# Pooled attention and two dense stages on one core: copy and load order on the DMA queue, GpSimd's split order, two tiles transposed in fp32

## The chip, the cores and the metric

The kernel runs as one program on one core of a Trainium2 chip. The metric is the device time of one execution in microseconds; the number to predict is the median of several executions of the changed kernel, and of the kernel before three executions are known.

## What is computed

The reference is a chain of three layers on float32 inputs. Only the first one is touched by the change.

```python
def _attn_ref(q, k, v):                       # q, k, v: (2, 8, 1152, 64)
    B, H, S, D = q.shape
    factor = 2
    scale = 1.0 / np.sqrt(D)
    q_pool = q.reshape(B, H, S // factor, factor, D).mean(axis=3)
    scores = scale * np.matmul(q_pool, k.transpose(0, 1, 3, 2))
    scores = scores - np.max(scores, axis=-1, keepdims=True)
    attn = np.exp(scores)
    attn = attn / (np.sum(attn, axis=-1, keepdims=True) + 1e-09)
    return np.matmul(attn, v).astype(np.float32)
...
    x = _moe_ref(x=x, **moe_kwargs)           # x*tanh(softplus(x)) between two matmuls, 512 -> 2048 -> 512
    return _moe2_ref(x=x, **moe2_kwargs)      # 8 experts 512 -> 1024 -> 512, mixed by 8 Sinkhorn rounds
```

## The kernel before

The 16 heads are taken as 8 **pairs** of heads (`NPAIR`). A pair has 2 x 576 pooled queries, that is 9 **tiles** of 128 queries (`QTL`), and one turn of the loop at L665 is one **step** `g`: pair `p = g // 9`, step `t = g % 9` of the pair. fp32 precision is kept by splitting an operand into a rounded fp32r part ("hi") and the rest ("lo"), and by multiplying both.

A step has this chain over the engines. TensorE (PE) computes the scores of tile `g` (L448); VectorE (DVE) copies them, negated, out of the only score buffer in PSUM into a buffer `e` (3 of them) and finds the row maximum on the way (L453); ScalarE (ACT) takes the exponential in place (`exps`, L463). `hand_over(g)` (L465) then copies `e`, 128x1152 fp32, by DMA into a buffer `er` of type fp32r (2 of them). Three steps later (`LAG`) `transposes` turns `er` on PE in nine 128x128 blocks (L510), ACT writes the hi part (`eth`, L513) and DVE the lo part (`etl`, L516). Two to four tiles make a group, whose product with V is run in portions of 9 matmuls a step (L531). In order of the program, step `g` holds: the scores of `g`, GpSimd's preparations (`prep`), the first item of `turn(p, t)`, the transposes of tile `g - 3`, `hand_over(g - 1)`, the portion of the product with V, the other items of `turn`, and `exps(g)`. At its end come `loads` (L704), one entry of `late` (L706), and the weight work that is due (`run_all`).

The next pair's operands are prepared beside this. `prep(p, t)` issues GpSimd's (POOL's) work by the table `PREP` (L587): `q0` to `q3` pool, scale and split the next pair's queries, `v..` and `k..` split V and K, head by head, hi (`..0`) and lo (`..1`). A finished split appends the load of the next raw tile to `loads`, since it frees the raw tile's only buffer: `q3` the load of the queries, a lo split that of K or V. `trans_q(p, u)` turns split queries on PE (L428), ACT copies them to `qT` (L430), and `swap` (L418) writes by two DMAs the copy of `qT` with its two halves of partitions exchanged; the middle tile has a buffer of its own, `qz`, which is swapped too. When a pair's output is complete, `late` gets `scale_x(p)`: five transposes of the reciprocal row sums, two multiplications on DVE (L554), and on POOL the split of the pair's output `xs` into `xh` and `xl` (L560, L561), four instructions.

All DMAs are issued by SyncE (SP), one after the other in the order of the program. An issue that has to wait for another engine holds all later issues.

Steps 0 to 2 (`g < LAG`) are written apart (L672 to L680): they have no transposes, and the copies of tiles 0 and 1 are handed over in steps 1 and 2. From step 73 on (`T0`) the second layer's matmuls (L219, L752) run interleaved with the rest of the attention; after it follow the experts (L1013, L1171).

Of the kernel before, what the change touches and what calls it, by code (L numbers as in the profile page):

```python
# [8 lines left out]
F32 = mybir.dt.float32  # L9
F32R = mybir.dt.float32r  # L10
# [13 lines left out]
def pool_attention_mish_sinkhorn_kernel(  # L24
# [261 lines left out]
    with ExitStack() as actx:  # L286
# [37 lines left out]
        def heads(p):  # L324
            b, hp = divmod(p, HPB)
            return b, hp, 2 * hp
# [91 lines left out]
        def swap(t):  # L418

            for a, b in ((0, D), (D, 0)):  # L420
                nc.sync.dma_start(out=t[a:a + D, :, 1, :].bitcast(F32), in_=t[b:b + D, :, 0, :].bitcast(F32))

        def trans_q(p, u):
            ps = ps_t.tile([P, 4, P], F32R, tag="t", name=f"psq{p}_{u}")
            t, _ = q_tile(p, 4 * u)
            n = min(4, QTL - 4 * u)
            for i in range(n):
                nc.tensor.transpose(  # L428
                    ps[:, i, :], qst[p][:, 4 * u + i, 0:2, :].rearrange("p a d -> p (a d)"), identr)
            nc.scalar.activation(t[:, :, 0, :], ps[:, 0:n].bitcast(F32), AF.Copy)  # L430
            swap(t)
            if 4 * u == MID:
                middle(p, ps, 1)
                swap(qz[p % 2])

        scS, eS, erS, rsS, rxS = {}, {}, {}, {}, {}

# [19 lines left out]
        def exps(g):  # L457
            p, t = divmod(g, QTL)
            sc, nm = scS.pop(g)
            e = eS[g] = sc.rearrange("p a b -> p (a b)")  # L460
            if t == 0:
                rsS[p] = tiny.tile([P, QTL], F32, tag="rs", name=f"rs{p}", bufs=2)
            nc.scalar.activation(e, e, AF.Exp, bias=nm, scale=-1.0, accum_out=rsS[p][:, t:t + 1])  # L463

        def hand_over(g):  # L465

            e = eS.pop(g)
            er = erS[g] = er_p.tile([P, S], F32R, tag="er", name=f"er{g}")
            nc.sync.dma_start(out=er.bitcast(F32), in_=e)
# [26 lines left out]
        def transposes(g):  # L496
            p, t = divmod(g, QTL)
            e = erS.pop(g)
            q0 = t * P
            parts = []  # L500
            for gi, (j, s0, n) in enumerate(GROUPS):
                a, b = max(q0, s0), min(q0 + P, s0 + n)
                if a < b:
                    parts.append((get_et(p, gi), a - q0, b - q0, a - s0))
            for c3 in range(3):
                pt = ps_t.tile([P, 4, P], F32R, tag="t", name=f"psT{g}_{c3}")
                ps = pt.bitcast(F32)
                for i in range(3):
                    c = 3 * c3 + i
                    nc.tensor.transpose(pt[:, i, :], e[:, c * P:(c + 1) * P], identr)  # L510
                cs = slice(3 * c3, 3 * c3 + 3)
                for (eh, el), a, b, o in parts:
                    nc.scalar.activation(eh[:, cs, o:o + b - a], ps[:, 0:3, a:b], AF.Copy)  # L513

                for (eh, el), a, b, o in reversed(parts):
                    nc.vector.tensor_tensor(  # L516
                        out=el[:, cs, o:o + b - a], in0=ps[:, 0:3, a:b],
                        in1=eh[:, cs, o:o + b - a].bitcast(F32), op=ALU.subtract)
            for gi, (j, s0, n) in enumerate(GROUPS):
                if q0 < s0 + n <= q0 + P:  # L520
                    queue_av(p, gi)

        def queue_av(p, gi):
            j, s0, n = GROUPS[gi]
            eh, el = et.pop((p, gi))
            box = {}

            def mm(c, which):
                if "ps" not in box:
                    box["ps"] = ps_a.tile([P, 512], F32, tag="av", name=f"psA{p}_{gi}")  # L530
                nc.tensor.matmul(  # L531
                    box["ps"][:, 0:n], lhsT=vst[p, j][:, c].rearrange("p a d -> p (a d)"),
                    rhs=(el, eh)[which][:, c, 0:n],
                    start=(c == 0 and which == 0), stop=(c == NK - 1 and which == 1))

            def evac():
                ps = box["ps"]
                b, hp, h0 = heads(p)
                t = o_p.tile([D, SQ - c0], F32, tag="t", name=f"avt{p}_{gi}")
                nc.scalar.activation(t[:, 0:n], ps[D:2 * D, 0:n], AF.Copy)  # L540
                s = s0 - j * (SQ - D)
                nc.vector.tensor_tensor(
                    out=xs[j * D:(j + 1) * D, s:s + n], in0=ps[0:D, 0:n], in1=t[:, 0:n], op=ALU.add)
                if gi == len(GROUPS) - 1:
                    late.append(lambda: scale_x(p))

            def scale_x(p):
                for i0, n in ((0, 4), (4, 1)):
                    ps = ps_t.tile([P, n, P], F32, tag="t", name=f"psr{p}_{i0}", padded_shape=[P, 4, P])
                    rx = rxS[i0]  # L550
                    for i in range(n):
                        nc.tensor.transpose(ps[:, i, :], rx[:, i].rearrange("p a d -> p (a d)"), ident)
                    x = xs[:, i0 * P:(i0 + n) * P]
                    nc.vector.tensor_tensor(out=x, in0=ps.rearrange("p a b -> p (a b)"), in1=x, op=ALU.mult)  # L554
                b, hp, h0 = heads(p)
                sl = slice(b * SQ, (b + 1) * SQ)
                for j in range(2):
                    r = slice(j * D, (j + 1) * D)
                    x = xs[r, j * D:j * D + SQ]
                    split_hi(nc.gpsimd, xh[r, hp, sl], x)  # L560
                    split_lo(nc.gpsimd, xl[r, hp, sl], x, xh[r, hp, sl])  # L561

            for c in range(NK):
                for w in range(2):
                    av_todo.append(lambda c=c, w=w: mm(c, w))
            av_todo[-1] = lambda: (mm(NK - 1, 1), evac())
# [13 lines left out]
        for m in range(1, 2 * NG1 - 1):  # L580
# [4 lines left out]


        PREP = {  # L587
            "q0": 1, "q1": 2, "q2": 3, "q3": 5, "v00": 1, "v01": 2, "v10": 4, "v11": 7,
            "k00": 3, "k01": 4, "k10": 6, "k11": 8,
        }  # L590
        PREP0 = {"k00": 3, "k01": 3, "q0": 4, "q1": 4, "q2": 5, "q3": 5, "v10": 5, "v11": 7, "k10": 7, "k11": 8}
        TURN = {"k0": (5, 6, 7), "k1": (2, 3, 3), "k10": (0, 0, 2), "q0": (2, 2, 3), "q": (6, 1, 2)}
# [72 lines left out]
        for g in range(T0 + EARLY):  # L665
            p, t = divmod(g, QTL)
            if g == 1:
                bctx.close()
                ps_t = pool("ps_t", 4, space=PSUM)
                ps_a = pool("ps_a", 1, space=PSUM)  # L670
            pre = turn(p, t) if g < NQ else []
            if g < LAG:  # L672
                exps(g)
                for f in pre:
                    f()
                if g:
                    hand_over(g - 1)
                if g + 1 < LAG:
                    split_kv(0, 0, "v", nc.gpsimd, g)
                    scores(g + 2, ps_s)  # L680
            else:
                if LAG < g < NQ:
                    scores(g)
                if p and g < NQ:
                    prep(p, t)
                if g < T0:
                    run(g, "dve")
                if p and t == 1:
                    row_sums(p - 1)
                if pre:  # L690
                    pre.pop(0)()
                ready = len(av_todo)
                if g < NQ + LAG:
                    transposes(g - LAG)
                if g <= NQ:
                    hand_over(g - 1)
                if not p:
                    prep(p, t)
                run_av(min(ready, 9 if g < NQ else 18))
                for f in pre:  # L700
                    f()
                if g < NQ:
                    exps(g)
            while loads:  # L704
                loads.pop(0)()
            if late:  # L706
                late.pop(0)()
            if g < T0:
                run_all(g)
            if g == QTL:  # L710
                load_gate()
            if g == NQ - 1:
                sctx.close()
                ps_o = ctx.enter_context(tc.tile_pool(name="ps_o", bufs=3, space=PSUM, side="right"))
                wpools["d0"] = ctx.enter_context(tc.tile_pool(name="wd0", bufs=1, side="right"))
                mctx = ExitStack()
                wpools["d1"] = mctx.enter_context(tc.tile_pool(name="wd1", bufs=1, side="right"))
                wpools["t"] = mctx.enter_context(tc.tile_pool(name="wt2", bufs=3, side="right"))
            if g >= T0:
                mish_step(g - T0)  # L720
        run_av(len(av_todo))
        for f in late:
            f()


    wpools[1] = mctx.enter_context(tc.tile_pool(name="wb", bufs=1, side="right"))
# [540 lines left out]
```

## Time and profile before

| | us |
|---|---|
| median of 3 executions (1259.51 to 1262.87) | 1260.65 |
| the profiled execution, its own time | 1258.57 |
| its span, first to last instruction | 1256.8 |

The span is cut into windows below; the attention fills about its first 300 us, and PE is busy through nearly all of what follows. In the profile a wait is the idle time of an engine just before an instruction, put down to the engine and line that came last. [...]

### The profile page before, as it was taken

How to read it: one execution, taken by the hardware profiler on the slowest of the kernel's cores; microseconds unless marked ns; L12 is line 12 of the kernel's file. 1: busy time of each engine (PE TensorE's matmuls, PEld its weight loads, DVE VectorE, ACT ScalarE, POOL GpSimd, SP SyncE). 2: the span in 40 equal slices, each digit the busy share in tenths (PEclk: the TensorE clock that was granted, in tenths of full speed). 3: DMA queues.
4: the chain of work that ended last, by engine and by line, in shares of the span. 5: the costliest groups of instructions: out<-in, count | busy, mean ns of one | idle time of the engine just before them, and what ended most of it. 6: DMA issues, size and time to landing. Idle time of an engine off the chain costs nothing.

```text
span 1256.8 us, 19465 instructions
## 1 busy us (share of the span) xinstructions
PE 1217.6 (97%) x6872; PEld 1125.8 (90%) x6872; DVE 858.3 (68%) x1596; ACT 600.3 (48%) x1372; POOL 634.4 (50%) x737
## 2 busy tenths in 40 slices
PE   7988888999999999999999999999999999999998
PEld 7988888999999999988899999888888999998887
DVE  5877778887544433578876766866876667866865
ACT  6877778786755443352333333333233333333331
POOL 5445566433443433355865555555556654555552
PEclk9999999999999999999999999999999999999999
DMA  5876676653322211001111111011111111110112
GB/s 195 260 231 209 217 245 213 236 198 140 117 84 85 84 60 34 18 9 51 43 51 52 51 51 51 23 46 42 51 52 42 51 51 51 51 44 28 40 50 76
DMA packets 66417, 115.64 MB, mean 92 GB/s; under 512 B 6928, under 2 KB 39440, under 8 KB 66320
## 3 DMA queue, kind: packets, MB, share of 16 engines
q1 hardware_dynamic: 66320, 114.40, 28.5%
q8 instruction: 55, 0.90, 0.3%
q14 instruction: 42, 0.34, 0.1%
HBM read 64.50 MB, written 2.36 MB: 53 GB/s over the span
## 4 chain that ended last, share of the span: by engine, by line
PE 86%; DVE 4%; DMA 3%; POOL 3%; ACT 2%; issue 1%; SPq 0%; DVEq 0%; POOLq 0%; ACTq 0%
PE po L1171 29%; PE c L1013 25%; PE ph L219 10%; PE po L752 8%; PE psA L531 4%; PE psS L448 4%; DMA er<-e 3%; PE psT L510 2%; DVE e L453 2%; POOL xl L81 1%; DVE etl L516 1%; POOL qst L81 1%; POOL xh L78 1%; ACT eth L513 1%; ACT e L463 1%
## 5 line engine op out<-in xcount | busy, mean ns | idle before, releaser
L81 POOL TENSOR_TENSOR wslotsl<-s,wslotsh 128x256 fp32r<-128x256 f32 x180 | 132.9, 747 | 237.6 <-ACT wslotsh L74 237.6
L1179 DVE SCALAR_TENSOR_TENSOR oacc<-po,Pm,oacc 128x512 f32<-128x512 f32 (+1 forms) x217 | 161.1, 746 | 103.3 <-PE po L1171 95.9
L1171 PE MATMUL po<-wdbl,hhall 128*128 128x512 f32 (+1 forms) x543 | 214.4, 395 | 0.0
L1171 PE MATMUL po<-wdbh,hlall 128*128 128x512 f32 (+1 forms) x543 | 214.1, 394 | 0.0
L1171 PE MATMUL po<-wdbh,hhall 128*128 128x512 f32 (+1 forms) x543 | 214.0, 394 | 0.0
L1030 ACT ACTIVATE t<-c 128x384 f32<-128x384 f32 x80 | 39.1, 489 | 247.2 <-PE c L1013 247.2
L1050 ACT ACTIVATE hhall<-c 128x384 fp32r<-128x384 f32 x180 | 88.7, 493 | 128.9 <-DVE c L1046 126.3
L453 DVE TENSOR_SCALAR_CACHE_REDUCE e<-psS 128x1152 f32<-128x1152 f32 x72 | 97.5, 1355 | 49.3 <-PE psS L448 34.4
L1171 PEld LDWEIGHTS po<-wdbh,hhall 128*128 128x128 f32 x543 | 102.0, 188 | 24.3
L1171 PEld LDWEIGHTS po<-wdbl,hhall 128*128 128x128 f32 x543 | 102.0, 188 | 23.3
L1171 PEld LDWEIGHTS po<-wdbh,hlall 128*128 128x128 f32 x543 | 102.0, 188 | 23.3
L81 POOL TENSOR_TENSOR wslotsl<-rawu,wslotsh 128x256 fp32r<-128x256 f32 x120 | 91.0, 773 | 51.3 <-ACT wslotsh L74 51.3
L516 DVE TENSOR_TENSOR etl<-psT,eth 128x384 fp32r<-128x384 f32 (+1 forms) x240 | 107.8, 507 | 6.8 <-ACT eth L513 6.8
L513 ACT ACTIVATE eth<-psT 128x384 fp32r<-128x384 f32 (+1 forms) x240 | 93.1, 476 | 24.6 <-PE psT L510 24.3
L1051 DVE SCALAR_TENSOR_TENSOR hlall<-c,hhall 128x384 fp32r<-128x384 f32 x180 | 98.9, 549 | 2.1
L1013 PE MATMUL c<-x2h,wslotsl 128*128 128x384 f32 x280 | 94.8, 338 | 0.0
L1013 PE MATMUL c<-x2h,wslotsh 128*128 128x384 f32 x280 | 94.5, 337 | 0.0
L1013 PE MATMUL c<-x2l,wslotsh 128*128 128x384 f32 x280 | 94.1, 336 | 0.0
L463 ACT ACTIVATE e<-e,nm 128x1152 f32<-128x1152 f32 x72 | 91.3, 1268 | 2.0 <-DVE e L453 1.3
L448 PE MATMUL psS<-kT,qT 128*128 128x384 f32 x384 | 82.4, 350 | 6.4 <-DVE e L453 6.4
L510 PE MATMUL psT<-identr,er 128*128 128x128 f32 x648 | 69.7, 251 | 18.1 <-DMA er<-e 15.4
L531 PE MATMUL psA<-etl,vst 128*128 128x256 f32 (+1 forms) x288 | 84.2, 315 | 0.5 <-DVE rs L473 0.5
(353 smaller groups left out, 3092.3 us busy)
## 6 DMA issues: line engine op xcount, KB each, us to landing
er<-e SPq DMA_DIRECT2D x72, 576.0 KB, 3.7
rawd<-in_moe_w_dram SPq DMA_DIRECT2D x60, 256.0 KB, 2.8
rawu<-in_moe_w_dram SPq DMA_DIRECT2D x30, 384.0 KB, 3.3
raw<-in_moe_w_in_dram SPq DMA_DIRECT2D x16, 512.0 KB, 3.9
raw<-in_moe_w_out_dram SPq DMA_DIRECT2D x16, 512.0 KB, 3.7
vraw<-in_v_dram SPq DMA_DIRECT2D x16, 288.0 KB, 4.3
kraw<-in_k_dram SPq DMA_DIRECT2D x15, 288.0 KB, 4.6
qraw<-in_q_dram SPq DMA_DIRECT2D x7, 576.0 KB, 4.8
```

The costliest lines, as they stand in the source:

```text
L81: eng.tensor_tensor(out=lo, in0=src, in1=hi.bitcast(F32), op=ALU.subtract)
L219: nc.tensor.matmul(ps[:, 0:TH], lhsT=a, rhs=b, start=(n == 0), stop=(n == len(ops) - 1))
L448: nc.tensor.matmul(ps[:, kb, 0:TH], lhsT=a, rhs=kt[:, kb * TH:(kb + 1) * TH], start=(n == 0), stop=(n == len(ops) - 1))
L453: nc.vector.tensor_scalar(sc, ps[:, :, 0:TH], -1.0, None, op0=ALU.mult, op1=ALU.min, accum_out=nm)
L463: nc.scalar.activation(e, e, AF.Exp, bias=nm, scale=-1.0, accum_out=rsS[p][:, t:t + 1])
L513: nc.scalar.activation(eh[:, cs, o:o + b - a], ps[:, 0:3, a:b], AF.Copy)
L516: nc.vector.tensor_tensor(out=el[:, cs, o:o + b - a], in0=ps[:, 0:3, a:b], in1=eh[:, cs, o:o + b - a].bitcast(F32), op=ALU.subtract)
L531: nc.tensor.matmul(box["ps"][:, 0:n], lhsT=vst[p, j][:, c].rearrange("p a d -> p (a d)"), rhs=(el, eh)[which][:, c, 0:n], start=(c == 0 an ...
L752: nc.tensor.matmul(ps[:, 0:TH], lhsT=a, rhs=b, start=(n == 0), stop=(n == len(ops) - 1))
L1013: nc.tensor.matmul(cb[c], lhsT=a_, rhs=b_, start=FIRST[n] and m == 0, stop=LAST[n] and m == len(ops) - 1, skip_group_check=True)
L1171: nc.tensor.matmul(ps[:, 0:w], lhsT=a, rhs=b[:, cs], start=(n == 0), stop=(n == len(ops) - 1))
L1179: nc.vector.scalar_tensor_tensor(out=oa, in0=ps[:, 0:w], scalar=gate, in1=oa, op0=ALU.mult, op1=ALU.add)
```

## The change

It has four parts.

1. **Order on SP.** `swap` is no longer called where the queries are turned but appended to `loads`, and `loads` is emptied at the head of the next step instead of at the end of the same one. So a step's loads and swaps stand behind that step's `hand_over` and weight load, and ahead of the next step's `hand_over`.
2. **Order on POOL.** `q3` is due at step 4 of a pair instead of 5, `v10` at 5 instead of 4, `k10` at 7 instead of 6. The split of the output is cut off from `scale_x` as `split_x` and runs one step later.
3. **First two tiles.** For `g < 2` the exponential writes straight into an `er` buffer declared fp32; there is no `hand_over`, and the nine transposes of each use the fp32 identity.
4. Entries of `late` that are added while the last ones run are run as well.

```diff
-            swap(t)
+            loads.append(lambda: swap(t))
             if 4 * u == MID:
                 middle(p, ps, 1)
-                swap(qz[p % 2])
+                loads.append(lambda: swap(qz[p % 2]))
...
             sc, nm = scS.pop(g)
-            e = eS[g] = sc.rearrange("p a b -> p (a b)")
+            sc = sc.rearrange("p a b -> p (a b)")
+            if g < 2:
+                e = erS[g] = er_p.tile([P, S], F32, tag="er", name=f"er{g}")
+            else:
+                e = eS[g] = sc
...
-            nc.scalar.activation(e, e, AF.Exp, bias=nm, scale=-1.0, accum_out=rsS[p][:, t:t + 1])
+            nc.scalar.activation(e, sc, AF.Exp, bias=nm, scale=-1.0, accum_out=rsS[p][:, t:t + 1])
...
-                pt = ps_t.tile([P, 4, P], F32R, tag="t", name=f"psT{g}_{c3}")
+                pt = ps_t.tile([P, 4, P], e.dtype, tag="t", name=f"psT{g}_{c3}")
...
-                    nc.tensor.transpose(pt[:, i, :], e[:, c * P:(c + 1) * P], identr)
+                    nc.tensor.transpose(pt[:, i, :], e[:, c * P:(c + 1) * P], ident if g < 2 else identr)
...
                     nc.vector.tensor_tensor(out=x, in0=ps.rearrange("p a b -> p (a b)"), in1=x, op=ALU.mult)
+                late.append(lambda: split_x(p))
+
+            def split_x(p):
                 b, hp, h0 = heads(p)
...
-            "q0": 1, "q1": 2, "q2": 3, "q3": 5, "v00": 1, "v01": 2, "v10": 4, "v11": 7,
-            "k00": 3, "k01": 4, "k10": 6, "k11": 8,
+            "q0": 1, "q1": 2, "q2": 3, "q3": 4, "v00": 1, "v01": 2, "v10": 5, "v11": 7,
+            "k00": 3, "k01": 4, "k10": 7, "k11": 8,
...
             pre = turn(p, t) if g < NQ else []
+            while loads:
+                loads.pop(0)()
             if g < LAG:
                 exps(g)
                 for f in pre:
                     f()
-                if g:
-                    hand_over(g - 1)
...
-            while loads:
-                loads.pop(0)()
-            if late:
+            for _ in range(min(len(late), 2 if p >= NPAIR else 1)):
                 late.pop(0)()
...
-        for f in late:
-            f()
+        while late:
+            late.pop(0)()
```

The engines' rows differ as follows. DVE's order is the same row for row; ACT's differs only in the target of two exponentials, PE's only in the identity and the type of 18 transposes.

SP, from step 4 of pair 1 to step 1 of pair 2; `qraw`, `kraw`, `vraw` are raw loads, `raw` a weight, `er<-e` the copy that `hand_over` issues. Before:

```order
L469 DMA er_866<-e_777 128x1152
L332 DMA kraw_1_881<-in_k_dram 128x576
L469 DMA er_933<-e_842 128x1152
L340 DMA qraw_946<-in_q_dram 128x9x128
L469 DMA er_983<-e_903 128x1152
L421 DMA qT_0_998<-qT_0_998 64x4x128 x2
L469 DMA er_1049<-e_955 128x1152
L332 DMA vraw_0_1052<-in_v_dram 128x576
L469 DMA er_1084<-e_1014 128x1152
L332 DMA kraw_0_1097<-in_k_dram 128x576
L469 DMA er_1130<-e_1062 128x1152
L421 DMA qT_1_1169<-qT_1_1169 64x4x128 x2
```

The same stretch after:

```order
L473 DMA er_863<-e_775 128x1152
L340 DMA qraw_887<-in_q_dram 128x9x128
L332 DMA kraw_1_889<-in_k_dram 128x576
L473 DMA er_929<-e_840 128x1152
L473 DMA er_979<-e_898 128x1152
L421 DMA qT_0_994<-qT_0_994 64x4x128 x2
L473 DMA er_1047<-e_953 128x1152
L332 DMA vraw_0_1051<-in_v_dram 128x576
L473 DMA er_1082<-e_1010 128x1152
L332 DMA kraw_0_1096<-in_k_dram 128x576
L473 DMA er_1128<-e_1060 128x1152
L473 DMA er_1195<-e_1105 128x1152
```

The load of the queries stood between the copies of steps 5 and 6, behind `q3`; now it stands, with that of K, ahead of the copy of step 5. The swap of `qT_0` stood behind the copy of step 6 and stands there still, but belongs to step 7 now.

POOL, steps 3 to 8 of pair 1 (`qst`, `kst`, `vst` are the split operands; L78 is a hi part, L81 a lo part). Before:

```order
L78 TENSOR_SCALAR qst_780<-qraw_444 128x9x64
L78 TENSOR_SCALAR kst_0_782<-kraw_0_594 128x9x64
L78 TENSOR_SCALAR vst_1_845<-vraw_1_768 128x9x64
L81 TENSOR_TENSOR kst_0_782<-kraw_0_594,kst_0_782 128x9x64
L78 TENSOR_SCALAR xh<-xs 64x576
L81 TENSOR_TENSOR xl<-xs,xh 64x576
L78 TENSOR_SCALAR xh<-xs 64x576
L81 TENSOR_TENSOR xl<-xs,xh 64x576
L81 TENSOR_TENSOR qst_780<-qraw_444,qst_780 128x9x64
L78 TENSOR_SCALAR kst_1_958<-kraw_1_881 128x9x64
L81 TENSOR_TENSOR vst_1_845<-vraw_1_768,vst_1_845 128x9x64
L81 TENSOR_TENSOR kst_1_958<-kraw_1_881,kst_1_958 128x9x64
```

After:

```order
L78 TENSOR_SCALAR qst_778<-qraw_442 128x9x64
L78 TENSOR_SCALAR kst_0_780<-kraw_0_592 128x9x64
L81 TENSOR_TENSOR qst_778<-qraw_442,qst_778 128x9x64
L81 TENSOR_TENSOR kst_0_780<-kraw_0_592,kst_0_780 128x9x64
L78 TENSOR_SCALAR vst_1_901<-vraw_1_764 128x9x64
L78 TENSOR_SCALAR xh<-xs 64x576
L81 TENSOR_TENSOR xl<-xs,xh 64x576
L78 TENSOR_SCALAR xh<-xs 64x576
L81 TENSOR_TENSOR xl<-xs,xh 64x576
L81 TENSOR_TENSOR vst_1_901<-vraw_1_764,vst_1_901 128x9x64
L78 TENSOR_SCALAR kst_1_1014<-kraw_1_889 128x9x64
L81 TENSOR_TENSOR kst_1_1014<-kraw_1_889,kst_1_1014 128x9x64
```

The lo part of the queries (`qst`, L81) stood behind the four instructions on `xh` and `xl`; it now stands six rows further up, right behind the hi part of K.

SP at the start of the program, steps 0 to 5. Before:

```order
L340 DMA qraw_269<-in_q_dram 128x9x128
L469 DMA er_280<-e_218 128x1152
L332 DMA vraw_1_293<-in_v_dram 128x576
L469 DMA er_316<-e_234 128x1152
L469 DMA er_343<-e_264 128x1152
L332 DMA kraw_1_349<-in_k_dram 128x576
L469 DMA er_385<-e_290 128x1152
L469 DMA er_426<-e_364 128x1152
L340 DMA qraw_444<-in_q_dram 128x9x128
```

After:

```order
L340 DMA qraw_244<-in_q_dram 128x9x128
L332 DMA vraw_1_293<-in_v_dram 128x576
L473 DMA er_341<-e_269 128x1152
L332 DMA kraw_1_347<-in_k_dram 128x576
L473 DMA er_383<-e_290 128x1152
L473 DMA er_424<-e_362 128x1152
L340 DMA qraw_442<-in_q_dram 128x9x128
```

Two copies are gone, and the loads of V and K come one place further up.

## Rows read from the trace of the kernel before

**Rows 1.** The page: TensorE's busy share, and the copies' issues (count, KB, us to landing).
```profile
PE 1217.6 (97%) x6872; PEld 1125.8 (90%) x6872; DVE 858.3 (68%) x1596; ACT 600.3 (48%) x1372; POOL 634.4 (50%) x737
...
er<-e SPq DMA_DIRECT2D x72, 576.0 KB, 3.7
```

**Rows 2.** PE's waits: us in total, times, longest.
```profile
PE psT L510 <- DMA er<-e: 15.4, 6, 2.9
PE psq L428 <- POOL qst L81: 7.1, 6, 1.2
PE psS L448 <- DVE e L453: 6.9, 11, 1.5
```

**Rows 3.** Chain that ended last: start, length of the first score group of step 4, per pair.
```profile
52.17 2.16 PE psS L448 x12
...
237.92 2.20 PE psS L448 x12
...
271.47 2.19 PE psS L448 x12
```

**Rows 4.** Windows: start:end, length, busy of PE, PEld, DVE, ACT, POOL, then granted clock, DMA share.
```profile
20.00:52.00 32.00, 30.68 (x231) 29.87 (x232) 27.31 (x55) 27.27 (x62) 12.62 (x18) 0.95 0.75 238
52.00:89.00 37.00, 32.48 (x249) 31.27 (x248) 29.08 (x60) 29.09 (x65) 17.78 (x20) 0.95 0.69 226
238.00:271.40 33.40, 31.22 (x246) 29.96 (x246) 28.69 (x61) 28.68 (x66) 15.64 (x17) 1.00 0.65 223
```

**Rows 5.** Timeline of SP's DMA issues, pair 1, steps 5 to 7: start, length.
```profile
59.21 0.47 SPq L469 DMA_DIRECT2D er<-e  x1
64.64 0.39 SPq L340 DMA_DIRECT2D qraw<-in_q_dram  x1
65.22 0.47 SPq L469 DMA_DIRECT2D er<-e  x1
65.87 2.06 SPq L421 DMA_DIRECT2D qT<-qT  x2
```

**Rows 6.** Timeline of POOL, the same steps; in brackets the wait before and its releaser.
```profile
58.66 0.67 POOL L78 TENSOR_SCALAR xh<-xs 64x576 fp32r<-64x576 f32 x1 [2.76 <-DVE xs L554]
...
63.21 1.40 POOL L81 TENSOR_TENSOR qst<-qraw,qst 128x576 fp32r<-128x576 f32 x1
```

**Rows 7.** Timeline of PE, pair 1, steps 6 and 8.
```profile
64.67 0.54 PE L428 MATMUL psq<-identr,qst 128*128 128x128 f32 x4 [1.23 <-POOL qst L81]
...
71.58 1.35 PE L510 MATMUL psT<-identr,er 128*128 128x128 f32 x9 [2.46 <-DMA er<-e]
```

**Rows 8.** Timeline of PE, start of the program.
```profile
13.24 1.34 PE L448 MATMUL psS<-kT,qT 128*128 128x384 f32 x6 [1.46 <-DVE e L453]
...
14.62 1.01 PE L411 MATMUL psq<-identr,qst 128*128 128x128 f32 x10
18.54 0.94 PE L510 MATMUL psT<-identr,er 128*128 128x128 f32 x9 [2.91 <-DMA er<-e]
19.97 3.90 PE L448 MATMUL psS<-kT,qz 128*128 128x384 f32 x12 [0.49 <-DVE e L453]
```

**Rows 9.** Timeline of ACT at the start: the last copies of turned queries.
```profile
16.06 0.90 ACT L414 ACTIVATE qT<-psq 128x512 fp32r<-128x512 f32 x2
```

**Rows 10.** Timeline of DVE at the start: the row maximum of tile 3.
```profile
18.55 1.36 DVE L453 TENSOR_SCALAR_CACHE_REDUCE e<-psS 128x1152 f32<-128x1152 f32 x1 [5.37 <-DMA er<-e]
```

**Rows 11.** Timeline of SP at the start: the copy of tile 0.
```profile
12.65 0.62 SPq L469 DMA_DIRECT2D er<-e  x1
```

**Rows 12.** PE's groups by form: transposes of `er`, of the row sums, and fp32 matmuls at the start: busy, mean ns.
```profile
L510 PE MATMUL psT<-identr,er 128*128 128x128 f32 x648 | 69.7, 251 | 18.1 <-DMA er<-e 15.4 <-DVE xs L554 1.5 <-ACT kT L387 1.0
...
L552 PE MATMUL psr<-ident,rx 128*128 128x128 f32 x40 | 5.7, 272 | 0.0
...
L598 PE MATMUL psw<-ident 128*128 128x128 f32 x18 | 4.5, 437 | 1.4 <-POOL ident masks.py:199 1.4
```

**Rows 13.** Timeline of PE: step 4's twelve score matmuls in pair 1.
```profile
52.01 2.32 PE L448 MATMUL psS<-kT,qz 128*128 128x384 f32 x12
```

## The prediction

> **What bounds the kernel now.** First the page [rows 1]: TensorE is busy for 1217.6 of 1256.8 us, so all that can be won without taking away matmuls is its 39 us of idle time and the time that it spends at the lower clock. Then its waits [rows 2]: 15.4 us for copies of `er`, six times, 7.1 us for POOL's split of the queries, six times, and 6.9 us for DVE's row maximum. All three are in the attention, and they return pair by pair. Then the chain that ended last, at one point of each pair [rows 3]: the first scores of step 4 start at 52.17 and, five pairs later, at 237.92, that is 37.15 us a pair; the next one follows at 271.47, after 33.55 us. The window of that shorter pair shows the clock at 1.00 and TensorE busy for 31.22 us; a window of an ordinary pair shows 0.95 and 32.48 us [rows 4]. The shorter pair has no load of queries in it, since there is no pair left to load for, and no wait for a copy.
>
> Where the ordinary pair loses its time is read from three engines side by side. POOL starts on the pair's output at 58.66, four instructions, and reaches the lo part of the next queries only at 63.21; it ends at 64.61 [rows 6]. TensorE has waited 1.23 us for it when it turns the queries at 64.67 [rows 7]. SP has waited as well: after the copy at 59.21 its next issue is the load of the queries, which needs that same split, at 64.64; the next copy stands behind it and goes out at 65.22 [rows 5]. It lands just before 71.58, where TensorE has idled 2.46 us for it [rows 7], 6.4 us after its issue against a median of 3.7 us [rows 1], because the load and two swaps share the way with it. One late instruction on POOL thus costs two stalls.
>
> **What the change does, part by part.** The sum is made against the profiled execution, 1258.57 us; the median of the runs lies 2.1 us above it, and I carry the difference over to it.
>
> (1) The order on SP and POOL in the pairs. In the new order the lo part of the queries stands ahead of the output's split, behind K's hi part, and waits for nothing on DVE. On the times of [rows 6] it is done before POOL's wait of 2.76 us for DVE ends at 58.66, so some 6 us earlier than 64.61. The wait at 64.67 goes: 7.1 us in six pairs [rows 2]. The load of the queries goes out at the head of step 5, before the copy that left at 59.21; the copy behind it, now at 65.22, can leave as soon as its tile is ready and its buffer free, a step after 59.21; a step is 33.55 / 9 = 3.7 us [rows 3], so at about 62.9. TensorE would want it at 71.58 less both stalls, 67.9. With the median landing it is there at 66.6, with 6.4 us at 69.3, 1.4 us late. I take the median, because the load is now 3 us ahead of this copy, where it was 0.6 us ahead. The stall then goes, and with it the lower clock behind it: (37.15 - 33.55) x 5 = 18.0 us. Built from the parts it would be 15.4 - 2.9 = 12.5 us of waiting and 5 x (32.48 - 31.22) = 6.3 us of slower matmuls, 18.8 us; I take the smaller, which was measured whole.
>
> The output's split stays where DVE lets it start and loses its 1.40 us rider, so it ends no later; its reader is the next layer, and DVE's next write to `xs` is two steps off. `v10` and `k10` are read in the next pair; POOL has 17.78 us of work in 37.00 [rows 4]. The swaps are issued in the next step, ahead of a copy; two took 2.06 us on SP [rows 5]. That copy waits for the transposes of its own step anyway, which end 1.34 + 0.94 = 2.3 us into it (scores, then transposes, by the lengths in [rows 8]), so this costs nothing while ACT has written `qT` by the head of the step. Without that cover the copy would leave 2.06 us later, and against the 1.3 us that it has in hand at the median landing that is 0.8 us a pair. In the last pair POOL's order around the output does not change, so the start of the second layer keeps its distance: nothing.
>
> (2) The first two tiles. Before, TensorE ends the last turned queries at 14.62 + 1.01 = 15.63 and idles 2.91 us for the copy of tile 0, issued at 12.65 [rows 8, 11]. DVE has the same wait, 5.37 us, since tile 3 needs the buffer that the copy reads [rows 10]. Without copy both are gone. What comes next: the transposes need PSUM buffers that ACT empties until 16.96 [rows 9], the last one of the three at about 16.5, so they end at about 16.9. DVE can take the scores of tile 3 at 13.24 + 1.34 = 14.58 [rows 8] and is done at 15.9. The twelve score matmuls of step 4 start at 16.9 instead of 19.97: 3.1 us. They took 3.90 us at the lower clock [rows 8]; the same twelve take 2.32 us in pair 1 [rows 13]: 1.6 us, if the clock stays up.
>
> Against that stand 18 transposes in fp32, which the trace has not shown for this operand. The nearest row is a transpose of fp32 data by the same fp32 identity, 5.7 / 40 = 0.14 us busy each, against 69.7 / 648 = 0.11 us for the fp32r ones [rows 12]: 18 x 0.035 = 0.6 us. The far end is the fp32 matmul of the start, two records a call, 2 x 4.5 / 18 = 0.50 us [rows 12], which would make it 18 x 0.39 = 7.0 us. Below nothing I see no reason for a gain. I take 0.6 us, since that row is the same operation. Start: 3.1 + 1.6 - 0.6 = 4.1 us.
>
> [...] Priced like plain fp32 matmuls instead, the sum of the whole change would be 22.8 us.
>
> (3) What comes next in a pair. DVE has 29.08 us and ACT 29.09 us of work in a pair [rows 4]. With both stalls gone a pair takes 33.55 - 1.2 = 32.4 us, so both would be 90% busy in it. They are chained to TensorE by a single score buffer: the next scores wait until DVE has read the last ones. I cost this at nothing, because the waits for DVE now come to 6.9 us in all eight pairs [rows 2], though TensorE runs most of each pair without a stall already; the other end is in the rivals.
>
> Sum: 18.0 + 7.1 + 4.1 = 29.2 us. 1258.57 - 29.2 = 1229.4 for such an execution, and **1260.65 - 29.2 = 1231.4** for the median.
>
> **The rivals.**
>
> A. Copies stay late. The DMA share of a pair is 0.69 [rows 4]; the same bytes in 32.4 us make 0.79, and the load of queries and that of K now stand together ahead of a copy. For it: 6.4 us for one copy behind one load, and the 1.4 us found above. Against it: SP's hole from 59.68 to 64.64 [rows 5] is filled, so the transfers are spread. Price: a stall of 1.4 us in each of five pairs, too short to pull the clock down, since the shorter pair has 1.00 with a wait for the queries in it. 1231.4 + 7.0 = 1238.4.
>
> B. DVE or ACT takes over. No pair is seen shorter than 33.55 us [rows 3]. If that is their floor, the 7.1 us of the queries' split go into waits for DVE: 1231.4 + 7.1 = 1238.5.
>
> C. The clock falls at the start all the same. TensorE still idles between 12 and 17 us, if less, and what it does there is mostly transposes. Then 1.6 us of the start stay: 1233.0. [...]
>
> D. Slower. The loads at the head of a step hold SP when POOL is late. The load of V at the head of step 8 now waits for a lo part that stands behind the output's split. That split ends at 63.21 [rows 6], the lo part 1.4 us later, at 64.6. Step 8 would begin 1.3 us of scores ahead of its transposes at 67.9, so 2.0 us after that, and its copy waits for these transposes until 68.8. If POOL lagged by more than about 4 us, a copy would go out late at step 8, and one more at step 3, in the same way, in each of seven pairs: two stalls of the present size, 3.6 us each, against the one that goes. 1260.65 - 4.1 - 7.1 - 18.0 + 7 x 7.2 = 1281.9. Against it: POOL's share.
>
> E. It does not do what it says: the stall at 71.58 stays although SP is free, since the copy's own 6.4 us are the cause. Then only 7.1 + 4.1 us come: 1249.5.
>
> **How the numbers follow.** Forecast 0.60, A 0.13, B 0.11, C 0.10, D 0.03, E 0.03. The range is from 1226.5 (the remaining waits for DVE, 6.9 us, partly gone too, since the one after the stalled copy had the same cause) to 1239.5, B and the spread of the runs; what lies outside is D, E and tails, under 2 in 10. A change of 0.3%, 3.8 us, is about what a measurement of this kernel can tell from none. Faster by more than that are all cases but D, a little of each taken off: 0.95; same 0.02; slower 0.03.
>
> **What the next profile would show.** Right: no wait of TensorE for `er` above 1 us and none for `qst`; pairs of 32 to 33 us at a granted clock of 1.00; SP's longest hold no longer before a load of queries; the twelve matmuls of step 4 starting near 17 us. Wrong: a wait of the transposes in steps 7, 8 or 0 (A, E), longer waits of the scores for DVE (B), clock 0.50 around 17 to 21 us (C), SP holding before a load of V (D).

## The result and the profile after

| | before | after |
|---|---|---|
| median of 4 executions, us | 1260.08 | 1228.97 (1227.81 to 1231.68) |
| the profiled execution, us | 1258.57 | 1228.29 |
| its span, us | 1256.8 | 1226.4 |

The ratio of the medians is 0.9753, with an interval of 0.9729 to 0.9776. The gain is 31.1 us by the medians and 30.3 us by the profiled executions; 29.2 us had been forecast, 1231.4 us for the median. (A fourth execution of the kernel before lowers its median from 1260.65 to 1260.08 us.)

The page of after has TensorE busy for 8.8 us less than in [rows 1], though it computes the same. The granted clock, TensorE's as a share of full speed, has a mean of 1.000 over the span of after, where it was 0.991 over that of before: TensorE no longer spends time at the lower clock.

```profile
PE 1208.8 (99%) x6872; PEld 1117.6 (91%) x6872; DVE 859.4 (70%) x1596; ACT 599.0 (49%) x1372; POOL 635.8 (52%) x737
...
er<-e SPq DMA_DIRECT2D x70, 576.0 KB, 3.4
```

PE's waits answer to [rows 2]. The first two rows of before, for the copies and for the split queries, are gone, 22.5 us together; the wait for DVE's row maximum is nearly what it was, and the wait for `kT` has grown from 1.0 us [rows 12] to 2.0 us.

```profile
PE psS L448 <- DVE e L453: 6.1, 10, 1.5
PE psT L514 <- ACT kT L387: 2.0, 6, 0.4
```

The chain that ended last, at the point of [rows 3], now has that point in every pair. The first column is the start. The first row is step 4 of pair 0.

```profile
17.13 2.12 PE psS L448 x12
...
47.29 2.17 PE psS L448 x12
...
208.91 2.19 PE psS L448 x12
...
241.15 2.19 PE psS L448 x12
```

From 47.29 to 208.91 are five pairs of 32.32 us, against 37.15 us; the next one takes 32.24 us, against 33.55 us. The gain can be read off as it grows. At the twelve score matmuls of step 4 in pair 1 it is 52.01 - 47.13 = 4.88 us [rows 13]; at the row of 208.91 it is 29.0 us; at 241.15 it is 30.3 us; and at the end of the span 30.4 us. So 4.9 us come from the start, 24.1 us from five pairs, 1.3 us from the sixth, and nothing is given back by what follows.

The windows of a pair answer to [rows 4]: start:end, length, busy of PE, PEld, DVE, ACT, POOL, then the granted clock, the DMA share and GB/s. The clock is 1.00, DVE and ACT are busy for 92% and 91%, and the DMA share has risen from 0.69 to 0.84.

```profile
20.00:47.00 27.00, 26.05 (x212) 25.28 (x209) 24.87 (x51) 24.89 (x59) 11.64 (x17) 1.00 0.79 257
47.00:79.00 32.00, 30.96 (x249) 30.11 (x247) 29.36 (x61) 29.05 (x67) 20.09 (x23) 1.00 0.84 273
208.90:241.00 32.10, 31.03 (x247) 29.87 (x245) 28.82 (x61) 28.79 (x66) 15.48 (x18) 1.00 0.65 225
```

In pair 1, POOL splits the queries (`qst`, L81) at 47.52, ahead of the wait for DVE, and still starts on the output as soon as DVE lets it [rows 6].

```profile
47.52 1.44 POOL L81 TENSOR_TENSOR qst<-qraw,qst 128x576 fp32r<-128x576 f32 x1
...
53.78 0.67 POOL L78 TENSOR_SCALAR xh<-xs 64x576 fp32r<-64x576 f32 x1 [2.80 <-DVE xs L558]
```

SP issues the load of the queries at 50.82, right behind a copy, without a hold. The two copies of steps 5 and 6, which stood at 59.21 and 65.22 [rows 5], leave within one merged row of 3.65 us, the second of them at 57.51.

```profile
50.25 0.48 SPq L473 DMA_DIRECT2D er<-e  x1
50.82 0.54 SPq L340 DMA_DIRECT2D qraw<-in_q_dram  x1
51.41 1.64 SPq L332 DMA_DIRECT2D kraw<-in_k_dram  x1
54.33 3.65 SPq L473 DMA_DIRECT2D er<-e  x2
```

At the start, PE's timeline has the fp32 transposes (`psT<-ident`) where the idle time was, and step 4's matmuls take 2.35 us where they took 3.90 us [rows 8].

```profile
13.10 1.32 PE L448 MATMUL psS<-kT,qT 128*128 128x384 f32 x6 [1.46 <-DVE e L453]
...
15.32 0.51 PE L514 MATMUL psT<-ident,er 128*128 128x128 f32 x3
16.10 1.04 PE L514 MATMUL psT<-ident,er 128*128 128x128 f32 x6 [0.26 <-ACT qz L402]
16.89 2.35 PE L448 MATMUL psS<-kT,qz 128*128 128x384 f32 x12
19.08 1.15 PE L514 MATMUL psT<-ident,er 128*128 128x128 f32 x9
20.70 1.32 PE L448 MATMUL psS<-kT,qT 128*128 128x384 f32 x6 [0.47 <-DVE e L453]
```

The granted clock was 0.50 beside the 3.90 us and is 1.00 beside the 2.35 us. The first window is of before, the second of after, in the columns of [rows 4]:

```profile
21.00:22.00 1.00, 1.00 (x4) 1.00 (x4) 0.32 (x1) 0.50 (x2) 1.00 (x2) 0.50 1.06 369
```

```profile
17.00:18.00 1.00, 1.00 (x8) 1.00 (x7) 0.77 (x2) 1.00 (x4) 1.00 (x1) 1.00 0.10 19
```

### The profile page after: what moved, and what is told of

Its sections match the earlier page's. It is cut to its first block, busy times and chain, and to the rows that moved or that the text cites. A ratio compares the mean times of both kernels' runs of the same rounds, so it can differ in the third digit from the quotient of the medians.

```text
span 1226.4 us, 19436 instructions
## 1 busy us (share of the span) xinstructions
PE 1208.8 (99%) x6872; PEld 1117.6 (91%) x6872; DVE 859.4 (70%) x1596; ACT 599.0 (49%) x1372; POOL 635.8 (52%) x737
## 4 chain that ended last, share of the span: by engine, by line
PE 89%; DVE 8%; ACT 2%; issue 1%; POOL 0%; DVEq 0%; ACTq 0%; POOLq 0%
PE po L1176 30%; PE c L1018 26%; PE ph L219 10%; PE po L757 8%; PE psS L448 5%; PE psA L535 4%; DVE e L453 3%; DVE etl L520 3%; PE psT L514 2%; ACT eth L517 1%; ACT e L467 1%; DVE xs L546 1%; PE psk L386 1%; DVE xs L558 0%; PE psw L605 0%
## 5 line engine op out<-in xcount | busy, mean ns | idle before, releaser
L81 POOL TENSOR_TENSOR wslotsl<-s,wslotsh 128x256 fp32r<-128x256 f32 x180 | 132.9, 747 | 237.6 <-ACT wslotsh L74 237.6
L81 POOL TENSOR_TENSOR wslotsl<-rawu,wslotsh 128x256 fp32r<-128x256 f32 x120 | 91.0, 773 | 51.2 <-ACT wslotsh L74 51.2
L74 ACT ACTIVATE wslotsh<-s 128x256 fp32r<-128x256 f32 x180 | 72.0, 410 | 24.3 <-DVE s L984 24.3
L535 PE MATMUL psA<-etl,vst 128*128 128x256 f32 (+1 forms) x288 | 80.4, 303 | 0.5 <-DVE rs L477 0.5
```

The source lines that it names most:

```text
L81: eng.tensor_tensor(out=lo, in0=src, in1=hi.bitcast(F32), op=ALU.subtract)
L535: nc.tensor.matmul(box["ps"][:, 0:n], lhsT=vst[p, j][:, c].rearrange("p a d -> p (a d)"), rhs=(el, eh)[which][:, c, 0:n], start=(c == 0 an ...
```

## The experiments

Each experiment is told with its edit against the kernel before, or against the changed one where that is said. The median of before that stands beside a result is that of the same chip.

**The parts one by one.** My theory was that the order on POOL does the work in the pairs: one late instruction causes both stalls, and the queue is innocent. The main rival was the queue's own order.

*GpSimd's order alone.* The edit is the table of due steps, and `split_x` with its loops over `late`, as in the change.

```diff
-            "q0": 1, "q1": 2, "q2": 3, "q3": 5, "v00": 1, "v01": 2, "v10": 4, "v11": 7,
-            "k00": 3, "k01": 4, "k10": 6, "k11": 8,
+            "q0": 1, "q1": 2, "q2": 3, "q3": 4, "v00": 1, "v01": 2, "v10": 5, "v11": 7,
+            "k00": 3, "k01": 4, "k10": 7, "k11": 8,
...
+                late.append(lambda: split_x(p))
```

> The kernel before with GpSimd's order alone changed (the table of due steps, and the output's split one step later); loads and swaps as before. My theory: one late POOL instruction causes both stalls, so this alone removes the waits for the split queries and for the late copy, with the lower clock behind it: 1260.1 - 25.4 = 1234.7 us, pairs of about 32.4 us. Rival: the copy is late by its place behind loads and swaps on the queue; then only the 7.1 us of waits for the split queries go: 1253.0 us.

Measured: 1232.57 us against 1259.12, ratio 0.9794 (0.9774 to 0.9814), that is 26.5 us. PE's waits have one for a copy left, the one at the start, and none for the queries:

```profile
PE psS L448 <- DVE e L453: 6.7, 11, 1.5
PE psT L510 <- DMA er<-e: 2.3, 1, 2.3
```

*The queue's order alone.*

```diff
-            swap(t)
+            loads.append(lambda: swap(t))
...
             pre = turn(p, t) if g < NQ else []
+            while loads:
+                loads.pop(0)()
...
-            while loads:
-                loads.pop(0)()
             if late:
```

> The kernel before with the queue's order alone changed (loads emptied at the head of the next step, swaps among them); GpSimd's order as before. My theory: the load of the queries still waits for the split that stands behind the output's split, and the copy of step 6 still stands behind that load, so both stalls stay: 1260 us, within 2 us. Rival: the queue's order is what the copies need: the 18.0 us of the copies' stalls go and the 7.1 us stay: 1242.1 us.

Measured: 1256.36 us against 1259.12, ratio 0.9985 (0.9974 to 0.9996). Both stalls are there, and SP is held before the load of the queries as long as before. In the first fence are PE's waits; in the second is SP's own wait, with total, count and longest, first of this run and then of the kernel before:

```profile
PE psT L510 <- DMA er<-e: 13.9, 6, 2.6
PE psq L428 <- POOL qst L81: 7.2, 6, 1.2
```

```profile
SPq L340 <- POOL qst L81: 27.9, 6, 4.9
...
SPq L340 <- POOL qst L81: 27.6, 6, 4.9
```

The rival falls. The 2.8 us that it did gain by the medians (the ratio makes it 1.9 us) are more than I had allowed for; its span is 2.5 us shorter, 1.5 us of these already at step 4 of pair 1 (50.5 instead of 52.0); at the start the load of the queries left 0.8 us earlier than in the profile of before, behind the same two issues, so I do not put all of it down to the order. What this gain comes from stays open.

*The first two tiles alone.*

```diff
+            if g < 2:
+                e = erS[g] = er_p.tile([P, S], F32, tag="er", name=f"er{g}")
+            else:
+                e = eS[g] = sc
...
-                    nc.tensor.transpose(pt[:, i, :], e[:, c * P:(c + 1) * P], identr)
+                    nc.tensor.transpose(pt[:, i, :], e[:, c * P:(c + 1) * P], ident if g < 2 else identr)
...
-                if g:
-                    hand_over(g - 1)
```

> The kernel before with the first two tiles alone changed (exponential straight into an fp32 buffer, no copies of tiles 0 and 1, fp32 transposes). My theory: the start and the pairs are separate; the start gives back 4.9 us (the profile after has step 4 of pair 1 4.88 us earlier than before) and the pairs keep their 37.15 us: 1260.1 - 4.9 = 1255.2 us. Rival: the pairs run by transfers and POOL, not by TensorE, so the head start is waited away at the first late copy near 71 us: 1260 us.

Measured: 1253.55 us against 1259.12, ratio 0.9956 (0.9943 to 0.9968), 5.6 us. Most of the head start of the first tiles is kept through pairs that still stall: on the chain that ended last, step 4 starts 4.83 us earlier than before in pair 1 (47.34) and 3.83 us earlier in pair 7 (267.64).

**How little of the order is needed.** *One number.*

```diff
-            "q0": 1, "q1": 2, "q2": 3, "q3": 5, "v00": 1, "v01": 2, "v10": 4, "v11": 7,
+            "q0": 1, "q1": 2, "q2": 3, "q3": 4, "v00": 1, "v01": 2, "v10": 4, "v11": 7,
```

> The kernel before with one number changed: the lo part of the queries is due at step 4 instead of 5. My theory: that one instruction ahead of the output's split is all the pairs need: 1234.7 us, within 2 us of the whole change of GpSimd's order. Rival: the output's split has to be moved as well, since it makes V's and K's lo parts late and with them the loads at the end of steps 7 and 8: half of the gain at most, 1247 us or more.

Measured: 1233.00 us against 1259.12, ratio 0.9798 (0.9778 to 0.9817): 26.1 us, where the whole of POOL's part gave 26.5. The number moves two things: the instruction on POOL, and with it the load of the queries on SP, which now leaves ahead of the copy of step 5 (59.09):

```profile
55.53 0.59 SPq L340 DMA_DIRECT2D qraw<-in_q_dram  x1
```

So this run alone does not tell the two apart. The next one does.

*The output's split one step later, the table left alone* (`split_x` and `late` as in the change).

> The kernel before with the output's split alone moved one step later; the table keeps the queries' lo part at step 5, which now stands ahead of the split there. My theory: ahead of the split is enough, at whichever step; the same gain as by the table alone: 1233 us, within 2. Rival: the load of the queries now leaves at the end of step 5, only some 3 us ahead of the copy of step 6 instead of 6 to 7, and the copy lands 1.4 us late in five pairs: 1240 us.

Measured: 1232.48 us against 1257.70, ratio 0.9801 (0.9782 to 0.9820). So the queries' lo part has to stand ahead of the output's split; at which step does not matter, and neither do `v10` and `k10`. Here the load keeps its old place on SP, between the copies of steps 5 and 6; only the hold is gone:

```profile
58.54 0.47 SPq L469 DMA_DIRECT2D er<-e  x1
59.11 0.53 SPq L340 DMA_DIRECT2D qraw<-in_q_dram  x1
61.71 0.47 SPq L469 DMA_DIRECT2D er<-e  x1
```

The gain is the same, so it is POOL's order that counts, and not the load's place. The rival's late copy does come, but in one pair of five. In PE's timeline of that pair it is 1.54 us, where 1.4 us had been worked out:

```profile
194.89 1.31 PE L448 MATMUL psS<-kT,qT 128*128 128x384 f32 x6 [0.47 <-DMA er<-e]
197.75 0.92 PE L510 MATMUL psT<-identr,er 128*128 128x128 f32 x9 [1.54 <-DMA er<-e]
```

*The change without the queue's order* (against the changed kernel: loads emptied at the end of their step, swaps issued where the queries are turned).

> The changed kernel with the queue's order put back (loads emptied at the end of their step, swaps issued where the queries are turned). My theory: the queue's order is worth nothing once POOL is early; the same time as the changed kernel, 1229 us within 1.5. Rival: it is worth the 2.8 us that it gave alone: 1231.8 us.

Measured: 1228.63 us, against 1228.97 for the whole change, which was timed apart from it; the ratios to their own kernels before are 0.9769 (0.9750 to 0.9788) and 0.9753 (0.9729 to 0.9776). Once POOL is early, the queue's order is worth no time that can be told. It may leave a little more room: in the profiles two copies come 0.52 and 0.25 us late without it, and none with it.

**The start.** *The copy of tile 0 ahead of the load that it stood behind, no fp32 tiles.*

```diff
                 if g:
                     hand_over(g - 1)
+                if g == 1:
+                    while loads:
+                        loads.pop(0)()
...
-            while loads:
+            while len(loads) > (g == 0):
                 loads.pop(0)()
```

> The kernel before with one issue moved: the copy of tile 0 goes out ahead of the load of the next pair's queries, on which it stood waiting for POOL. No fp32 transposes. My theory: at the start as in the pairs the copy was late by the load ahead of it, which left at 12.22 us and needed POOL; ahead of it the copy leaves at about 11.7 us and lands in 3 us, before TensorE comes for it at 15.6 us; the same 4.9 to 5.6 us as without copies: 1254 us. Rival: the copy itself takes too long beside the first loads and has to be avoided: 1258 us or more.

Measured: 1254.51 us against 1257.70, ratio 0.9972 (0.9961 to 0.9984), 3.2 us by the medians and 4.6 us between the profiled executions (1254.00 and 1258.57). In SP's timeline the copy leaves at 11.03, and in PE's timeline nothing waits for it; 0.27 us remain for the copy of tile 1. The first fence has SP's row of before that stood ahead of [rows 11], the second the rows of this run.

```profile
12.22 0.38 SPq L340 DMA_DIRECT2D qraw<-in_q_dram  x1
```

```profile
11.03 0.51 SPq L469 DMA_DIRECT2D er<-e  x1
11.65 0.53 SPq L340 DMA_DIRECT2D qraw<-in_q_dram  x1
```

```profile
12.66 1.34 PE L448 MATMUL psS<-kT,qT 128*128 128x384 f32 x6 [1.46 <-DVE e L453]
...
14.90 0.42 PE L510 MATMUL psT<-identr,er 128*128 128x128 f32 x3
...
16.46 2.34 PE L448 MATMUL psS<-kT,qz 128*128 128x384 f32 x12
19.07 0.93 PE L510 MATMUL psT<-identr,er 128*128 128x128 f32 x9 [0.27 <-DMA er<-e]
```

So here too the copy was late by the load ahead of it on SP, which needed POOL: 12.65 against 11.03. The fp32 tiles avoid the copies; they are not needed for the gain.

*Both small edits together:* the one number and the copy ahead of the load.

> The kernel before with two small edits: the queries' lo part due at step 4 instead of 5, and the copy of tile 0 issued ahead of the load of the queries at the start. No other change to the queue, no fp32 tiles, the output's split in its old place. My theory: these two take the place of the whole change: 1229 us within 1.5. Rival: the copies of tiles 0 and 1 leave the 1 to 2 us at the start that the fp32 tiles do not have: 1231 us.

Measured: 1228.89 us against 1259.51, ratio 0.9755 (0.9741 to 0.9768). Two small edits, with the old order of swaps and without fp32 tiles, give what the whole change gives.

**What a stall costs.** *Dummy matmuls in the stall* (against the kernel before, before the transposes of step 8 in pairs 1 to 5; their result is overwritten).

```diff
+                if c3 == 0 and t == 5 and 1 <= p <= 5:
+                    for _ in range(4):
+                        nc.tensor.matmul(ps[:, 0, :], lhsT=ident, rhs=ident, start=True, stop=True)
                 for i in range(3):
```

> The kernel before with four more fp32 matmuls of 128 columns (about 0.5 us each by the start's rows, their result is overwritten) ahead of the transposes that wait 2.46 us for the late copy, in the five pairs that have that wait. Theory: the stall costs twice, 2.5 us of waiting and 1.26 us of slower matmuls behind it; the extra work stands inside the wait, so the copy lands no later, the clock stays up, and 5 x 1.26 = 6.3 us come back: 1252 us. Rival: the slower matmuls have nothing to do with the idle time: no gain, 1258 us, or the extra work is added where the wait ends, 1260 us.

Measured: 1252.10 us against 1259.51, ratio 0.9943 (0.9924 to 0.9963), 7.4 us. The kernel became faster by work that is thrown away. The copy is as late as before: the transposes start at 71.70, against 71.58 [rows 7]. But the matmuls behind them, up to 0.59 us each before, take 0.31 us, and the window of the pair shows 1.00 where [rows 4] has 0.95. The first fence is of the kernel before:

```profile
72.72 0.59 PE L531 MATMUL psA<-etl,vst 128*128 128x320 f32 x1
```

```profile
68.79 1.05 PE L510 MATMUL psT<-ident 128*128 128x128 f32 x8
71.70 0.97 PE L513 MATMUL psT<-identr,er 128*128 128x128 f32 x9 [1.86 <-DMA er<-e]
...
72.87 0.31 PE L534 MATMUL psA<-etl,vst 128*128 128x320 f32 x1
```

```profile
52.00:89.00 37.00, 33.09 (x261) 32.02 (x261) 30.04 (x62) 30.20 (x67) 17.82 (x21) 1.00 0.73 238
```

It does not hold in all five pairs. In pairs 1, 2, 3 and 5 the clock stays up, and the six score matmuls behind the wait take 1.04 to 1.06 us on the chain that ended last; in pair 4 it falls in spite of the dummies, they take 1.94 us, and that pair is 37.45 us long where pairs 1 to 3 take 35.93, 35.45 and 35.65 us:

```profile
178.73 0.96 PE L513 MATMUL psT<-identr,er 128*128 128x128 f32 x9 [1.80 <-DMA er<-e]
```

```profile
159.00:196.50 37.50, 33.66 (x256) 32.48 (x255) 29.56 (x62) 29.73 (x67) 20.18 (x22) 0.95 0.68 223
```

The four executions fall into the same order: 1250.20, 1251.46, 1252.73 and 1256.36 us at mean granted clocks of 0.999, 0.997, 0.997 and 0.993. So the dummies keep the clock up in most pairs but not surely. Where they do, they separate the two halves of a stall: about 2.5 us of waiting, and the slower matmuls behind it.

**What is left.** Two tries at the 0.47 us that TensorE still waits for DVE at step 8, both against the changed kernel. *K's transposes moved into step 7:*

```diff
-        TURN = {"k0": (5, 6, 7), "k1": (2, 3, 3), "k10": (0, 0, 2), "q0": (2, 2, 3), "q": (6, 1, 2)}
+        TURN = {"k0": (7, 7, 7), "k1": (2, 3, 3), "k10": (0, 0, 2), "q0": (2, 2, 3), "q": (6, 1, 2)}
```

> The changed kernel with the turning of the next pair's first K head moved, all three parts to step 7, where TensorE has no portion of the product with V and then waits 0.47 us for DVE's row maximum. Theory: 6 more transposes (0.4 us) fill that wait, 0.4 us in each of seven pairs: 1226 us. Rival: ACT's three copies of kT delay the exponentials there and the wait goes elsewhere: 1229 us or more.

Measured: 1236.29 us, ratio 0.9845 (0.9819 to 0.9870) to the kernel before; the changed kernel's is 0.9753, so this is slower than the changed kernel, by 7 us by the medians and by 12 us by the ratios. The transposes now wait for PSUM buffers that ACT and DVE have still to empty, two waits in one step, and in four pairs the clock falls to 0.50 behind them (the six matmuls of 127.47 take 2.25 us, where the six of 20.70 in the changed kernel took 1.32):

```profile
125.99 0.45 PE L386 MATMUL psk<-identr,kst 128*128 128x128 f32 x3 [0.80 <-ACT kT L387]
127.18 0.50 PE L386 MATMUL psk<-identr,kst 128*128 128x128 f32 x3 [0.74 <-DVE etl L520]
127.47 2.25 PE L448 MATMUL psS<-kT,qT 128*128 128x384 f32 x6
```

```profile
126.00:131.00 5.00, 4.26 (x23) 4.05 (x24) 2.92 (x7) 4.88 (x14) 4.92 (x5) 0.66 0.50 177
```

*Three matmuls of the product with V moved from step 6 to step 7:*

```diff
-                run_av(min(ready, 9 if g < NQ else 18))
+                run_av(min(ready, 18 if g >= NQ else 6 if t == 6 else 9))
```

> The changed kernel with the product with V dealt out otherwise at two steps of a pair: 6 of its matmuls in step 6 instead of 9, and the 3 left over in step 7, which had none and at whose end TensorE waits 0.47 us for DVE's row maximum. Theory: three matmuls (0.36 us) fill most of that wait in each of seven pairs: 2.5 us less than the changed kernel, 1226.5 us. Rival: the group's buffer is freed a step later, ACT's hi parts wait for it, and the wait goes elsewhere: 1229 us or more.

Measured: 1229.04 us, ratio 0.9760 (0.9743 to 0.9777), no better than the changed kernel. The wait for the row maximum falls from 6.1 to 2.3 us, and most of that comes up at two other places, 0.9 us more for `kT` and 2.3 us for `xs`, which the changed kernel's waits do not list:

```profile
PE psT L514 <- ACT kT L387: 2.9, 6, 0.6
PE psA L535 <- DVE xs L546: 2.3, 7, 0.3
PE psS L448 <- DVE e L453: 2.3, 3, 1.5
```

No version was found that beats the changed kernel by more than the measurement can tell.

## Why the prediction was right

**The reading of the bound held.** The two waits, with the lower clock behind one of them, are what was won in the pairs, and they fell together. The forecast had 18.0 us for the copies and 7.1 us for the queries, 25.1 us over six pairs; the starts of step 4 give 24.1 + 1.3 = 25.4 us. The claim that one late instruction on POOL costs two stalls is now shown: two different edits, which have in common only that this instruction comes to stand ahead of the output's split, give 26.1 and 25.2 us, one of them with the load of the queries in its old place on SP, and the queue's order by itself leaves both stalls in place.

**What was attributed too widely.** The forecast told the orders on SP and POOL as one part and did not say that SP's does not mend either stall by itself. The order rows could have shown it: without POOL's part the queries' lo part stays behind the output's split, and the load that needs it stays ahead of the copy of step 6. Behind POOL's part neither the place of the loads nor that of the swaps makes a difference that can be told.

**The copy's landing was right for a reason that was too weak.** The prediction took the median landing because the load would leave 3 us ahead of the copy of step 6. It leaves 6.7 us ahead, 50.82 against 57.51. In the split's run the two are 2.6 us apart, 59.11 against 61.71 and as much in the late pair, and there one copy of five is 1.54 us late. So the choice between the two landings held, but 3 us would not have been a safe distance.

**The clock behind a stall** was taken from a comparison of pairs, 1.26 us in each of five. The dummy matmuls gave 7.4 us where 6.3 us were expected, about 1.5 us a pair over the five, with an interval that holds both; in the profiled execution, 5.8 us faster than that of before, the clock stayed up in four of the five.

**The start was undersized**, 4.1 us against 4.88 us in the profiles, and this is most of what the forecast lacks. Step 4 began at 16.89 instead of 19.97, 3.08 us where 3.1 had been said, and its twelve matmuls took 2.35 us where 2.32 had been said. That makes 4.6 us, and they are there at the scores of step 5 (20.70 instead of 25.32); the last 0.3 us come later, before step 4 of pair 1, and what they come from is open. The term that failed is the 0.6 us for the fp32 transposes. Their price was nearly right, but it is not on the path. PE's groups by form show busy time and mean:

```profile
L514 PE MATMUL psT<-identr,er 128*128 128x128 f32 x630 | 68.2, 248 | 4.2 <-ACT kT L387 2.0 <-DVE xs L558 1.2
...
L514 PE MATMUL psT<-ident,er 128*128 128x128 f32 x18 | 2.7, 280 | 0.3 <-ACT qz L402 0.3
```

That is 2.7 / 18 = 0.15 us against 68.2 / 630 = 0.11 us. The first nine stand where ACT's copies set the pace anyway, the wait of 0.26 us at 16.10: from the scores of step 3 to those of step 4 TensorE takes 16.89 - 13.10 = 3.79 us with them, and 16.46 - 12.66 = 3.80 us with fp32r ones in the run that only moves the copy. Behind the second nine TensorE waits for DVE, now 0.47 us at 20.70 where it was 0.74 us before:

```profile
25.32 1.31 PE L448 MATMUL psS<-kT,qT 128*128 128x384 f32 x6 [0.74 <-DVE e L453]
```

**The rivals.** A did not come: the DMA share rose to as much as 0.84 in a pair, above the 0.79 that had been worked out, and PE waits for no copy. It is real where the load leaves a step later, with 1.54 us in one pair of the split's run. Its price also rested on a sentence that does not hold in general, that short waits leave the clock up: in the kernel with K's transposes moved, the clock fell to 0.50 behind two waits of 0.80 and 0.74 us. B did not come as priced, the pairs went below 33.55 us; but it names what is next, since the two tries at the remaining wait only moved it, with DVE and ACT at 92% and 91% of a pair. C did not come: the clock was 1.00 from 12 to 24 us. Whether it matters to the clock that TensorE's work there is mostly transposes is not shown: score matmuls stand between them, and no run isolates it. D and E did not come: SP's hold before the load of the queries is 3.3 us, once, at the start, and PE waits for no copy at steps 7, 8 or 0. The sign that was named for D did show, SP held before a load of V, but only twice, 4.8 us together and 3.1 the longest, and no copy behind it came late.

## What to carry to other kernels

Where one queue issues everything in order, look for the issue that waits for a compute engine, and then for what stands ahead of that engine's instruction: here a one-step change in a table of due times was worth 26 us, while reordering the queue itself was worth 2 to 3 us alone, and nothing that could be told behind the other. A stall of TensorE behind which the clock falls is to be priced with the slower matmuls as well, here a further 1.3 to 1.5 us on 2.5 us. Before a copy is designed away, try to issue it one place earlier.

## What the runs showed of the hardware

The length of a wait did not by itself tell whether the clock falls. It stayed at 1.00 in the kernel with dummy matmuls behind a wait of 1.86 us and fell in the same execution behind one of 1.80 us, to 0.95 over the pair; in the split's run it stayed at 1.00 behind one of 1.54 us. In the kernel with K's transposes moved it fell to 0.50 in four pairs, of which three have a wait of 0.79 to 0.84 us and one of 0.74 us 1.2 us later, and stayed at 1.00 in an earlier pair with waits of 0.78 and 0.74 us. What decides between these is open.

The dummy fp32 matmuls of 128 columns were cheaper than the start had led me to expect: the eight records of four calls at 68.79 span 1.05 us together, 0.26 us a call, where 0.5 us a call had been taken from the first records of the program. The granted clock is given as 1.00 in both stretches; why the first records are longer is open. The prediction's far end for the fp32 transposes, and the 22.8 us that follow from it, rest on the dearer price: against 0.26 us a call, the 0.15 us that was measured is less by a factor of 1.8.
